# A planned single-core kernel: new fetch durations in its planner, score products that write whole PSUM banks, and a new table of priorities

## The chip, the cores and the metric

The kernel runs on one core of a Trainium2 chip. The metric is the device time of one execution in microseconds (us). A profiled execution gives its own span, from the first to the last instruction of the program. TensorE is PE in the profile, its weight loads are PEld, VectorE is DVE, ScalarE is ACT, GpSimd is POOL, and SyncE, which issues most of the transfers, is SP.

## What is computed

A retention layer (attention without softmax, with a decay for each head) is followed by two matrix products with a gate between them. There are 8 batches, 8 heads, 576 positions and 64 numbers a head, and the middle of the second part is 2048 wide. All inputs and the output are float32.

```python
scores = scale * np.matmul(q, k.transpose(0, 1, 3, 2))
Dmat = np.where(rel >= 0, gamma[:, None, None] ** rel[None, :, :], 0.0)
attn_out = np.matmul(scores * Dmat[None, :, :, :], v)
x = attn_out.transpose(0, 2, 1, 3).reshape(B * S, H * D)
h = x @ w_in
g = h * np.cos(h)
return (g @ w_out).astype(np.float32)
```

## The kernel before, in words

**The work.** The 4608 tokens are cut into 9 tiles of 512. A tile is made of two units of attention; a unit is one batch and a stretch of its positions, all 8 heads. For a unit `unit` loads k, q and v and casts them to bf16 (the decay is multiplied into q and v there, line 605), `scores` makes the products of keys and queries in PSUM and multiplies them with a triangle (line 714, on DVE), `states` adds keys times values to a running state, and `outputs` makes the attention result that becomes the tile's `xt`. All matmuls of attention are of 64 rows by 64 columns, in four lanes of the array; `emit_lanes` strings them into one task and line 675 issues them.

The first product of tiles 0 to 3 is `mlp1` (line 879), with a sine on ACT (line 888) and the gate on DVE (line 891). In tiles 4 to 8 (`SEVEN`) it is `seven1` (line 1008), which makes the same product from seven block products instead of eight, and the second product is `wino2` (line 1148) in all tiles, by the same scheme. In `seven1` one of the accumulations does not start from zero: ACT writes the first product into another PSUM bank (`seed`, line 939) and PE adds onto it.

**Marked banks.** The kernel keeps a flag for each of the 8 PSUM banks, `whole`: it is set when the last PE task that wrote the bank wrote all of it after one start. A seed that gets a bank without the flag has a dummy matmul of 512 columns put in front of it (`mark`, line 494); the planner counts 213 ns for it (`MARK`) and prefers a bank with the flag among those that are free (line 343). Before the change a score task starts anew with each of its products, so its banks don't get the flag.

**The planner.** The order of all instructions on all five engines is worked out when the kernel is built, by a list scheduler (`Graph.run`). Each task has an engine, a duration, the buffers that it needs and a priority. In each round every engine offers the task that could start first; among those within 60 ns (PE) or 40 ns (the others) of that, the lowest priority number goes (lines 300 to 302). The order found is emitted with the semaphore waits that the data need. The planned times themselves aren't emitted: an instruction starts on the chip as soon as its engine reaches it and its semaphores are there. This holds for SP's and POOL's transfers too, which stand in the order that the planner gave them.

Three pieces of the planner matter here. `FETCHES` holds, for stretches of planned time, how long a block of 256 PE instructions takes to arrive: PE asks for block k when it has seen 128 + 256k instructions and can't pass 443 + 256k before the block is there (lines 279 to 282). `SHIFT` is a string: each three characters say how many tasks to go on and what to add to that task's priority, in steps of 10 ns between -40.5 and +40.5 us (`shift`, line 226). And where the plan holds a gap of more than 400 ns on PE, while the bank for it is still free, dummy matmuls are emitted to fill it (`warm`, line 500); this ends with the first `mlp1` task of tile 1.

A task of attention is called `ses/` (scores), `ses:` and `ses+` (outputs). Going to one from another kind of task costs 95 ns in the plan, leaving one 105 ns, and one task of attention draws the next with a bonus of 2000 ns (`ENTER, LEAVE, BOND`).

Of the kernel before, what the change touches and what calls it, by code (L numbers as in the profile page):

```python
# [11 lines left out]
B, H, S, D = 8, 8, 576, 64  # L12
DM, DFF = H * D, 2048
# [6 lines left out]
NT = 72  # L20
# [79 lines left out]
def ap(t, size, p0, n, off, *dims):  # L100
    return bass.AP(t, p0 * size + off, [[size, n]] + [list(d) for d in dims])
# [29 lines left out]
class Graph:  # L131
# [54 lines left out]
    @staticmethod  # L186
    def fetch(at):
        return next(f for end, f in Graph.FETCHES if at < end)

    FETCHES = ((30000, 11500), (55000, 9500), (68000, 10200), (104000, 7800), (118000, 13000), (205000, 8800), (1e9, 6500))  # L190
    MARK = 213
    ENTER, LEAVE, BOND = 95, 105, 2000

# [181 lines left out]
class Kernel:  # L375
# [10 lines left out]
    SLABS = ((0, 'q', 0, 100), (2, 'q', 1, 101), (1, 'k', 1, 102), (3, 'k', 1, 103))  # L386
    NEXT = 2
    SHIFT = (
        "$|KLw3?#U,,G3(j'Xw'Q/$X((Oe$6_6w'8cY/cu/am-@X&h2/fT&^Z)u,'bK'Z/$Zt$X5)W0%Wo$Si)LO&Q8)V?&GC&>H&Xd&J="
        "&_;%hW$BL&Jk&Q#(Y3$CR&Ec&R3&I_&jf&Gz)Fi,Ul)X(&H\\%L3&V6'U{(R|$T'&K6&[,%Ev-0w%mf%hO'oe$fT$CQ%pN(^l+EV"  # L390
        "$8I*--'%V$=d$:1%=@$=-$Xp&.:$21&Yx$tv%kW$nq+wV*Sm)B_/?^&Ej)9[&,4&>V&LX&Wy)X+$Jj%ED$JH$WK&YT$1A)*k,#k"
        "$_*&3I+S^)PL$-y&9s$c%&-w(JS$<|&]L'LL'M.;=A&D<&;3&#`);o,Y`&U`._`,Yp'-@%VS$`j%$$$Y+<B=$N7'dd'c%$KF&;b"
        "$fO'U`,I99^#'Ym)ND'E*$FW%Jk%F\\.2@,sT$aT)W>(^T%T_'[Q.80&N0,/B-^B$A{%\\J&:0%CC-Vp+Ao,0z%i-%#U$+D%X-'Vi"
        "%XA$Bd%SJ&^d$Z#$JA)Sk'?#$@B)@;/66$F]&3H%-)%5r&+/%.q'DM&Zp0TU2M.&A\\&q-*Tc(D5'4P%Pu$5^%UZ*%M(9P$9a';>"
        "*g{-\\Z'Wt&\\K?kt&VZ'MP%p9(%B8GP(I''8c%.#$\\f(Z*;Y15J6(>n$Aa*B|*\\Y:Yg$R;%Vb$7e&_R,&i0dx6\\S'AW*E\\%Xx%RH"
        "(XU(4Z&:S7Wo.So&Se,^[&Xc-`K$L\\%Wp$XH$T++Zd'U<*|K.Y7,Mb'Ar&#b%S_%To%\\p$J\\%=#'7E$fZ$)'(/G%.<(7U)Qx$k6"
        "&2]&.U':a$2Y%8O%$b'=S'BS-_0$XW)L8$Z=+-j$,w6|C$|K9xJ"
    )
    GATE = 'k'
    TXENG = ("pool", "dve", "pool", "dve")  # L400
# [276 lines left out]
    def scores(self, u, prio, todo, split, extra=(), join=None):  # L677

        t, rem = self.tiles[u], u[1] == 2 or self.fine(u)
        kt, qt = t["kt"], t["qt"]  # L680
        N, ny = (64, 1) if rem else (128, 2)
        phases = []
        for cc in range(1 if rem else 2):
            lanes = {q: [] for q in self.LANES}
            sc, pt = [Buf("bk"), Buf("bk")], Buf("pt")
            t["pt", cc] = pt
            for r, s in self.LANES:
                n = 0
                for c in range(4) if rem else (2 * cc, 2 * cc + 1):
                    for y in range(2):  # L690
                        def rhs(r=r, s=s, c=c, y=y):
                            o = c * 128 + 64 * s
                            return ap(self.at(qt), 1024, 64 * r, 64, o + 512 * y, [1, 64]) if rem else ap(
                                self.at(qt), 1024, 64 * r, 64, o, [512, 2], [1, 64])
                        lanes[r, s].append((N, self.mm(
                            lambda r=r, s=s, n=n, sc=sc: ap(self.at(sc[r]), 512, 64 * s, 64, n * N, [1, N]),
                            lambda r=r, s=s, c=c, y=y: ap(self.at(kt), 1024, 64 * r, 64, y * 512 + c * 128 + 64 * s, [1, 64]),
                            rhs)))
                        n += 1
            reads = [(x, y) for x in (kt, qt) for y in range(2)]  # L700
            writes = [(b,) for b in sc]
            phases.append((lanes, reads, writes, []))
        for v, s in todo:
            self.states(v, s, *phases[-1][:3])
        if join is not None:
            join.append((u, phases))
            if len(join) < 2:
                return
            self.emit_lanes("ses/%d.%d" % u, prio, [x for _, y in join for x in y], alloc=[self.tiles[v]["pt", 0] for v, _ in join])
        for cc, ph in enumerate([[x] for x in phases] if split else [phases] * (join is None)):  # L710
            self.emit_lanes("ses/%d.%d" % u, prio + cc * split, ph, alloc=[t["pt", cc + x] for x in range(len(ph))])
        for b, pt, r in [(x[2][r][0], self.tiles[v]["pt", cc], r) for v, y in join or [(u, phases)]
                         for cc, x in enumerate(y) for r in range(2)]:
            self.one("dve", 610, lambda e, r=r, b=b, pt=pt: e.tensor_tensor(  # L714
                ap(self.at(pt), 1024, 0, 128, 512 * r, [64 * ny * ny, 8 // ny // ny], [1, 64 * ny * ny]),
                ap(self.at(b), 512, 0, 128, 0, [64 * ny * ny, 8 // ny // ny], [1, 64 * ny * ny]),
                ap(self.TR[ny], 64 * ny * ny, 0, 128, 0, [0, 8 // ny // ny], [1, 64 * ny * ny]), ALU.mult),
                r=[(b,)] + [("tr", ny, y) for y in range(ny)], w=[(pt, r)])
        for v, s in todo:
            self.snap(v, s)  # L720
        for i, more in enumerate(extra):
            alone = ({q: [] for q in self.LANES}, [], [], [])
            for v, s in more:
                self.states(v, s, *alone[:3])
            self.emit_lanes("ses=%d.%d" % u, prio + (split or 1000 * (i + 1)), [alone])
            for v, s in more:
                self.snap(v, s)
# [594 lines left out]
```

## Time and profile before

| | us |
|---|---|
| time, median of 3 runs | 284.11 (283.97 to 285.01) |
| profiled execution, span | 282.1 |
| PE busy | 274.2 |
| DVE busy | 226.7 |
| ACT busy | 174.9 |
| POOL busy | 152.8 |

The granted TensorE clock was 1.000 over the whole span. The transfers moved 49.90 MB. The busy time of an engine is the union of its instructions' spans. PE's matmuls are pipelined: the mean time of one matmul of 256 columns is 273 ns, but eight of them in a row took 0.87 us, so counts times distance, and not counts times mean, is what a row of matmuls costs. The seconds column of a table by windows is the length of the window; after it stand the busy times of the engines with their number of instructions.

### The profile page before, as it was taken

To read this page: it belongs to the slowest core of one execution; us is meant where nothing else is said; L and a number is where in the kernel's file an instruction comes from. 1 tells how busy PE (TensorE), PEld (TensorE's weight loads), DVE (VectorE), ACT (ScalarE), POOL (GpSimd) and SP (SyncE) were. 2 spreads that over 40 slices of the span, in tenths; PEclk is the share of its full clock that TensorE was granted. 3 is DMA by queue.
4 is the path that set the end of the run, shared out by engine and by line. 5 is a ranking of instruction groups with operands and counts; after the bars stand their busy time and mean duration, and the time that the engine had idled before them with its cause. 6 is when DMAs were issued, how large, how long until landed. Compare 5 with 4: busy or idle time off the path is not lost.

```text
span 282.1 us, 9696 instructions
## 1 busy us (share of the span) xinstructions
PE 274.2 (97%) x4088; PEld 216.5 (77%) x4088; DVE 226.7 (80%) x389; ACT 174.9 (62%) x355; POOL 152.8 (54%) x170
## 2 busy tenths in 40 slices
PE   7899999999999999999999999999999999999995
PEld 2567576888784476458888888888888889888884
DVE  4677979989937898898969786889689979579753
ACT  4357683672446744764578767785778577777620
POOL 5452870487334745258587949783779333433410
PEclk9999999999999999999999999999999999999999
DMA  7999999999999999999999999997857002200124
GB/s 194 265 224 279 244 179 228 283 199 193 192 260 224 207 188 258 188 200 188 293 159 260 184 244 207 231 208 169 169 145 151 3 2 77 77 0 2 74 77 149
DMA packets 133130, 49.90 MB, mean 177 GB/s; under 512 B 105440, under 2 KB 128992, under 8 KB 133088
## 3 DMA queue, kind: packets, MB, share of 16 engines
q1 hardware_dynamic: 128576, 44.84, 74.1%
q0 software_dynamic: 4224, 4.19, 9.3%
q8 instruction: 32, 0.52, 0.8%
q10 hardware_dynamic: 288, 0.26, 0.3%
q14 instruction: 10, 0.08, 0.1%
HBM read 36.70 MB, written 9.44 MB: 164 GB/s over the span
## 4 chain that ended last, share of the span: by engine, by line
PE 83%; DMA 8%; DVE 5%; POOL 1%; issue 1%; ACT 0%; SPq 0%; DVEq 0%
PE bk L1148 37%; PE bk L1008 22%; PE bk L879 14%; PE bk L675 8%; DMA stgv<-in_v_dram 3%; DMA wout<-in_moe_w_out_dram 3%; DVE pt L714 2%; DMA stgq<-in_q_dram 1%; PE bk L629 1%; PE bk L500 1%; DVE tw L1057 1%; POOL natv L605 1%; DVE gt L891 1%; DVE s L1079 1%; DVE s L1085 0%
## 5 line engine op out<-in xcount | busy, mean ns | idle before, releaser
L997 POOL TENSOR_TENSOR gt<-sq,cb 128x512 bf16<-128x512 f32 x40 | 46.1, 1161 | 38.5 <-ACT cb L993 24.6
L879 PE MATMUL bk<-xt,win 128*128 128x256 bf16 (+1 forms) x352 | 61.5, 321 | 0.2
L888 ACT ACTIVATE cb<-bk 128x256 bf16<-128x256 f32 (+1 forms) x88 | 41.7, 480 | 24.8 <-PE bk L879 22.6
L891 DVE TENSOR_TENSOR gt<-bk,cb 128x256 bf16<-128x256 f32 (+1 forms) x88 | 46.3, 542 | 12.5 <-ACT cb L888 8.5
L605 POOL TENSOR_TENSOR qnat<-stgq,wq 128x512 bf16<-128x512 f32 x32 | 33.5, 1051 | 39.8 <-DVE s L1079 19.9
L605 POOL TENSOR_TENSOR natv<-stgv,wv 128x512 bf16<-128x512 f32 x36 | 37.8, 1055 | 18.9 <-PE bk L675 4.3
L879 PEld LDWEIGHTS bk<-xt,win 128*128 128x128 bf16 x352 | 32.8, 98 | 19.3 <-ACT xt L555 0.8
L1148 PE MATMUL bk<-tw,s 128*128 128x256 bf16 x288 | 36.2, 273 | 0.4 <-ACT os L555 0.2
L1148 PE MATMUL bk<-wout,gt 128*128 128x256 bf16 x288 | 36.1, 273 | 0.3 <-DMA wout<-in_moe_w_out_dram 0.3
L1148 PE MATMUL bk<-wout,s 128*128 128x256 bf16 x288 | 35.9, 273 | 0.0
L997 DVE TENSOR_TENSOR gt<-bk,cb 128x512 bf16<-128x512 f32 x40 | 27.3, 687 | 9.5 <-ACT cb L993 6.9
L1008 PE MATMUL bk<-xt,win 128*128 128x256 bf16 x240 | 34.9, 273 | 0.0
L991 DVE TENSOR_TENSOR sq<-bk,sq 128x512 f32<-128x512 f32 x40 | 27.0, 686 | 9.3 <-ACT sq L555 4.3
L714 DVE TENSOR_TENSOR pt<-bk,tr 128x512 bf16<-128x512 f32 x48 | 30.7, 682 | 2.5 <-PE bk L675 2.4
L993 ACT ACTIVATE cb<-sq 128x512 bf16<-128x512 f32 x40 | 25.0, 630 | 11.3 <-DVE sq L991 11.0
L1148 PEld LDWEIGHTS bk<-tw,s 128*128 128x128 bf16 x288 | 28.0, 98 | 4.5 <-DVE tw L1057 0.3
L555 ACT ACTIVATE sn<-bk 128x512 f32<-128x512 f32 (+1 forms) x29 | 16.2, 565 | 24.0 <-PE bk L1148 22.2
L1148 PEld LDWEIGHTS bk<-wout,s 128*128 128x128 bf16 x288 | 27.6, 98 | 4.3 <-DVE gt L891 0.2
L1148 PEld LDWEIGHTS bk<-wout,gt 128*128 128x128 bf16 x288 | 27.7, 98 | 3.8 <-DMA wout<-in_moe_w_out_dram 0.5
L993 ACT ACTIVATE cb<-bk 128x512 bf16<-128x512 f32 x40 | 23.9, 600 | 8.6 <-PE bk L1008 7.2
L556 POOL CAST natk<-stgk 128x512 bf16<-128x512 f32 x34 | 20.9, 627 | 13.7 <-DMA stgk<-in_k_dram 8.4
L1137 DVE TENSOR_TENSOR os<-bk,sn 128x512 f32<-128x512 f32 (+1 forms) x28 | 18.5, 665 | 10.1 <-PE bk L1148 9.0
(80 smaller groups left out, 428.4 us busy)
## 6 DMA issues: line engine op xcount, KB each, us to landing
out_dram<-os SPq DMA_DIRECT2D x16, 512.0 KB, 4.6
stgq<-in_q_dram SPq DMA_DIRECT2D x20, 256.0 KB, 5.1
stgv<-in_v_dram SPq DMA_DIRECT2D x20, 256.0 KB, 5.0
stgk<-in_k_dram SPq DMA_DIRECT2D x20, 256.0 KB, 5.5
stgq<-in_q_dram SPq DMA_DIRECT2D x6, 512.0 KB, 6.9
stgk<-in_k_dram SPq DMA_DIRECT2D x6, 512.0 KB, 6.9
stgv<-in_v_dram SPq DMA_DIRECT2D x6, 512.0 KB, 7.2
win<-in_moe_w_in_dram POOLq DMA_DIRECT2D x4, 512.0 KB, 8.5
```

Source lines behind the costliest of these rows:

```text
L556: return self.one(eng, dur, lambda e: e.tensor_copy(dst(), src()), r=r, w=w, port=eng == "pool", **kw)
L605: self.one(eng, 610 if eng == "dve" else 1030, lambda e, out=out, inp=inp, tab=tab, col=col, hs=hs: e.tensor_tensor(out(), inp(), ap(tab, ...
L675: return lambda e: e.matmul(out(), lhs(), rhs(), start=start, stop=True, skip_group_check=True)
L714: self.one("dve", 610, lambda e, r=r, b=b, pt=pt: e.tensor_tensor(ap(self.at(pt), 1024, 0, 128, 512 * r, [64 * ny * ny, 8 // ny // ny], [1 ...
L879: inst = e.matmul(ap(self.at(bk), 512, 0, 128, 0, [1, n]), ap(self.WIN, 4 * DFF, 0, 128, c * DFF + 128 * f, [1, 128]), ap(self.at(xt), 204 ...
L888: self.one("act", n - 15, lambda e: e.activation(ap(self.at(cb), TB, 0, 128, 0, [1, n]), ap(self.at(bk), 512, 0, 128, 0, [1, n]), AF.Sin, ...
L891: self.one("dve", 75 + n / 0.96, lambda e: e.tensor_tensor(ap(self.at(gt), NF * TB, 0, 128, f * TB + 256 * h0, [1, n]), ap(self.at(bk), 51 ...
L991: self.one("dve", 610, lambda e: e.tensor_tensor(half(src), self.at(bank).ap(), half(src), ALU.add), r=[(bank,)], w=four(src))
L993: self.one("act", 530 if name else 490, lambda e: e.activation(self.at(cb).ap(), ap(self.at(src), size, 0, 128, 0, [1, 512]), AF.Sin, bias ...
L997: self.one(eng, 1120 if name else 610, lambda e: e.tensor_tensor(ap(self.at(gt), NF * TB, 0, 128, (8 * n + 2 * g) * TB + 256 * h, [TB, 2], ...
L1008: inst = e.matmul(ap(self.at(bank), 512, 0, 128, 256 * f, [1, 256]), l(c, f), rr(c), stop=True, skip_group_check=True, start=(first and f ...
L1148: inst = e.matmul(place(bank, tt), l(f, tt), rr(f), stop=True, skip_group_check=True, start=(first and f == 0 and tt < len(bank)))
```

## The change

Three things are edited. The durations of the planner's fetches are set to four stretches in place of seven:

```diff
-    FETCHES = ((30000, 11500), (55000, 9500), (68000, 10200), (104000, 7800), (118000, 13000), (205000, 8800), (1e9, 6500))
+    FETCHES = ((30000, 11500), (55000, 10200), (205000, 8600), (1e9, 6300))
```

The score products start a bank with the first product of each lane alone (`n == 0`) and write the others without a start; their tasks hand their banks over as `whole`, in the joined form for all but the banks of the running state:

```diff
-        phases = []
+        phases, banks = [], []
...
                         lanes[r, s].append((N, self.mm(
                             lambda r=r, s=s, n=n, sc=sc: ap(self.at(sc[r]), 512, 64 * s, 64, n * N, [1, N]),
                             lambda r=r, s=s, c=c, y=y: ap(self.at(kt), 1024, 64 * r, 64, y * 512 + c * 128 + 64 * s, [1, 64]),
-                            rhs)))
+                            rhs, start=n == 0)))
                         n += 1
             reads = [(x, y) for x in (kt, qt) for y in range(2)]
             writes = [(b,) for b in sc]
+            banks += sc
             phases.append((lanes, reads, writes, []))
...
-            self.emit_lanes("ses/%d.%d" % u, prio, [x for _, y in join for x in y], alloc=[self.tiles[v]["pt", 0] for v, _ in join])
+            self.emit_lanes("ses/%d.%d" % u, prio, [x for _, y in join for x in y], alloc=[self.tiles[v]["pt", 0] for v, _ in join],
+                            whole=[k[0] for _, y in join for x in y for k in x[2] if k[0] not in self.ST])
         for cc, ph in enumerate([[x] for x in phases] if split else [phases] * (join is None)):
-            self.emit_lanes("ses/%d.%d" % u, prio + cc * split, ph, alloc=[t["pt", cc + x] for x in range(len(ph))])
+            self.emit_lanes("ses/%d.%d" % u, prio + cc * split, ph, alloc=[t["pt", cc + x] for x in range(len(ph))], whole=banks)
```

And the string `SHIFT` is another one. The old one has 281 entries, up to task 1445; the new one has 1450, up to task 1450, one for nearly every task. The values of both lie between about -40 and +40 us; their standard deviation is 18.6 us in the old and 20.3 us in the new.

```diff
     SHIFT = (
-        "$|KLw3?#U,,G3(j'Xw'Q/$X((Oe$6_6w'8cY/cu/am-@X&h2/fT&^Z)u,'bK'Z/$Zt$X5)W0%Wo$Si)LO&Q8)V?&GC&>H&Xd&J="
...
+        "#B+$@($Pc$\\8$[#$M&$K8$MM$Gy$P*$j3$b/$he$bI$ML$\\|$Sb$|*$S<$I($l?$P%$m6$VJ$W%$bp$::$?A$]]$aQ$Ox$;'$P:$>)$PI"
...
     )
```

No instruction is added, removed or resized by these edits, but for the dummy matmuls, which the planner's result decides. What the new priorities decide is the order on each engine, the order of the transfers, and which of a pool's buffers each task gets.

More of the change, by code (lines that the diff above doesn't have):

```diff
@@ L388 @@
     SHIFT = (
-        "$|KLw3?#U,,G3(j'Xw'Q/$X((Oe$6_6w'8cY/cu/am-@X&h2/fT&^Z)u,'bK'Z/$Zt$X5)W0%Wo$Si)LO&Q8)V?&GC&>H&Xd&J="
[L390 to L397, printed above, removed]
+        "#B+$@($Pc$\\8$[#$M&$K8$MM$Gy$P*$j3$b/$he$bI$ML$\\|$Sb$|*$S<$I($l?$P%$m6$VJ$W%$bp$::$?A$]]$aQ$Ox$;'$P:$>)$PI"
@@ new lines @@
+        "$Ad$5Y$PY$[M$I-$|6$S4$>S$e&$Q$$c?$Kv$ci$V@$J{$JO$`p$^t$Hx$e7$4F$#-$|s$#`$8K$VN$KH$Em$>A$Ae$SB$Y)$P@$Mh$|="
+        "$V<$Sv$\\7$Rp$Tt$SL$Y-$Xs$E`$<i$K($Xw$KB$@n$*:$:q$In$U/$EQ$zb$hU$3b${D$K)$Al$Zv$HJ$Rm$#g$@J$a`$Cr$RJ$\\S$#-"
+        "${C$<q$hP$6c$X5$H:$RC$O($?1$ZB$R]$WI$'<$U;$d*$+r$p5$R+$8L$Hv$a1$bX$<\\$l5$#-$Zn$kO$Sp$;A$XT$'&$)\\$FN$5Y$_R"
+        "$E($Ml$A.$9x$c1$C)$[H$9]$.'$,<$@9$9w$+M$4=$,5$#6$WO$-y$ki$=`$)Y$EK$r_$E9$L&$Vo$3T$Ed$oF$Ef$Fk$gk$)w$`j$xF"
+        "$k?$aw$i$$iE$J>$^G$UD$D\\$Fp$TG$Mc$b#$'-$*l$N<$*+$It$DE$`1$F.$)z$=f$P5$cZ$i($Cv$c{$Ak$cU$#j$j=$g6$XO$St$Tm"
@@ new lines @@
+        "$`|$SQ$eL$^P$Wv$,\\$V8$Rc$zD$]=$cv$AW$Li$0n$Wo$k;$n7$Y1$<S$Ng$:^$Qs$`-$kV$ES$|&$0J$D=$Y)$F%$)u$>,$U]$?z$PV"
+        "$=d$lF$.h${e$8I$])$d-$O5$,+$8.$HS$Bh$Mm$.($2%$4?$1#$Iu$7E$?^$,r$SB$`c$lW$Ui$Q=$]_$7s$aH$`N$]r$c;$QF$'{$#0"
+        "$kM$T_$EO$KE$|r$MZ$aK$Lz$Q$$\\W$'3$bl$Nh$Qb$/k$?m$)3$RM${Z$9:$.a$=v$D{$VB$S:$7Y$X[$V2$#-$zZ$rS$E#$8j$/`$a="
+        "$Iy$Qr$Y&$ie$S?$s8$kj$Oq$VP$N'$*;$>Y$>o$uk$L3$WM$Iy$P.$@y$gC$ff$W&$>P$<v$ZO$K5$_1$^6$aV$j%$[n$e>$S&$0X$P+"
+        "$ZG$L_$Yu$`-$V:$zS$b`$l)${w$bD$@n$|s$'($hi$`,$-o$oH$)B$e[$TA$NB%JR$AQ$S]$\\+$fz$Cm$.P$LZ$RV$6l$k$$f)$>/$Y,"
@@ new lines @@
+        "$-_$d+$4S$Ur$gT$RQ$LI$$%$Y>$?8$6c$C@$3i$Db$JG$Ai$;{$9?$Fg$?m$5d$B,$q<$Z>$g[$T$$#-$[h$0X$Pk$W=$A-$BB$NU$3#"
+        "$M0$^;$CC$^A$8;$Y|$_m$*+$?Y$K]$[]$aC$a[$:m$2N$QB$84$up$Da$+n$H`$X<${$$B7$&6$IC$fO$3W$53$cy$-@$8v$LO$BY$lV"
+        "$x\\$hA$jn$cF$W1$Wz$s)$#-$Dp$zx$`x$AG$dX$Re$^5$A2$+L$<`$#3$)L$)4$Ly$w%$O/$DU$GK$d`$|s$-S$R|$Iu$[:$1>$]U$&$"
+        "$Ji$d\\$q9$Lf$@8$Z`$[3$y>$a:$[+$\\9$W%$U.$b`$0q$Oo$1I$OY$a]$X{$<<$?k$R{$cD$qG$R7$cD$[B$V'$])$QE$5J$H5$Vl$,L"
+        "$v|$0r$=i$HT$Cr$EI$hJ$dA$wK$c0$[5$Vl$V7$(q$AO$Vq$[]$4'$|)$DO$=%$u*$b4$0_$hD$3H$C1$\\?$@N$JV$K\\$.N$XK$f-$h="
@@ new lines @@
+        "$M%$_<$=-$OT$K[$Kj$NT$eZ$@P$(D$Xq$9&$gG$CJ$=S$Su$=v$U6$9m$lT$Iq$.Q$gL$GO$^{$Zh$oM$E@$yG$P|$RW$2,$vi$?)$Ej"
+        "$a4$(W$@X$K7$z3$YB$EB$j_$Kz$V\\$<9$a:$LB$|s$4@$^%$i{$]r$[:$`-$E5$@s$N5$rq$8>$<A$W*$ng$F;$[S$0k$<)$I6$A6$KO"
+        "$D`$M7$OG$WF$I*$F*$X,$DY$B.$Pp$]N$\\f$OW$J%$Sa$K1$]8$Y|$ZY$]F$X=$E3$DU$S[$c]$r/$v2$8m${|$nr$`6$Rv$gC$\\e$o7"
+        "$xL$Cj$QB$@U$^*$vH$PM${r$tn$Sm$Ki$:$$0^$YM$#-$b)$mh$CI$ns$\\i$5W$Yi$TQ$1x$f[$\\6$SS$6C$V/$Wf$:0$Lt$dq$Ma$I6"
+        "$qh$fg$se$Wr$`,$cn$Ou$pd$l8$zV$W.$ZR$l)$g[$KI$Ud$bV$:&$::$f8$XO$ik$w,$eS$mE$HM$T/$n'$*U$Z\\$jo$mf$QU$bR$q["
@@ new lines @@
+        "$Nq$RY$jl$F&$ZU$sc$CU$1Y$26$2t$#@$W\\$B8$f/$n8$@-$8t$-f$XU$z1$[>$Nb$tK$mT$5R$4h$]K$Pv$V:$MO$Q1$z?$/s$Y8$ZQ"
+        "$n3$|X$HS$W#$wP$[0$ps$9t$[h$Ea$C$$\\6$0)$f>$z9$=V$:h$Ul$M-$d$$]e$_A$$2$mc$gH$54$gN$t,$I)$U\\$[#$RZ$hh$d/$NP"
+        "$wx$g6$2($qR$4|$ag$i0$Kk$uj$#-$Y@$u;$_n$p:$<\\$jv$=j$GI$3T$Dl$m/$z^$56$|^$#9$^k$8z$yy$@_$O]$Sb$2$$S)$qG$=x"
+        "$T=$Qb$6q$FT$Xy$=K$TO$p,$KZ$ld$GP$P*$Du$fS$S@$5($Bv$e[$$f$N#$G+$vG$45$:1$Y?$?x$w,$)0$C;$JQ$;%$tA$L9$k_$Bf"
+        "$<F$x`$cA$AC$Vc$HI$^4$NU$sC${m$;8$J2$ba$x'$iL$N[$L%$iE$he$)^$>M$m@$1|$:/$v1$hZ$l|$DE$L/$Gw$?K$;\\$wc$lx$@H"
@@ new lines @@
+        "$,F$^m$*3$c8$`;$#2$E-$0A$M*$U2$I.$Y%$w6$ZO$ar$X+$yz$Xz${y$jt$9m$]#$4U$GF$Fp$dJ$go$H*$?u$@B$cf$SD$qh$x6$hC"
+        "$dY$74$p|$B]$C+$^;$Wa$\\:$Ru$>B$W{$V($a[$Ss$Os$F8$58$U+$OV$Xd$KA$CA$Bw$\\h$Vo$J3$F<$ck$M8$KT$BM$Rr$bp$_,$Ip"
+        "$VY$ER$fo$^W$RD$_u$IK$LW$Wz$Ha$da$=%$LP$]H${5$;k$#-$[6$AM$XK$'q$v^$KA$^?$qc$\\G$|d$>e$1`$)>$ka$>W$O%$4e$0+"
+        "$IT$QN$Q{$;_$;G$HC$+9$+a$.n$Ar$a.$uI$kD$/q$QA$TC$`a$/\\$pF$6d$^@$Bf$O]$pC$5/$[[$;=$Q{$'d$<i$C?$MA$CL$[D$hc"
+        "$sP$?n$??$g%$wF$.m$]d$cA$`#$IQ$_d$G7$vB$t{$G_$qN$O=$<L$7/$@:$j0$J^$?n$^+$>9$DR$@[$s]$Cg$SX$ph$Xn$K.$+i$YN"
@@ new lines @@
+        "$oX$TJ$a[$[k$f'$Xg$;%$m&$b*$$0$cu$1W$8-$y=$z;$04$$R$8R$U@$b`$6S$]E$Lr$f($cN$T7$ZP$|7$\\M$'$$B]$Sb$YK$z4$a&"
+        "$mH$rt$nH$iU$h?$[<$|s$|s$Db$-h$c.$5P$d%$@)$L%$ib$z#$vl$TF$k)$^_$@($?K$.E$-]$+*$uQ$nI$rr$Cb$VY$fR$wq$pS$:z"
+        "$jt$N,$04$y<$W3$|)$M|$Pp$|1$My$Gk$NA$8+$t[$8z$b+$d3$Pf$N@$z2$oP$6/$'m$Ve$8|$N($K;$1O$ON$+a$&2$Fv$O2$$^$U$"
+        "$r%$XC$&[$rl$4R$[m$8/$?t$g0$Y-$AI$NU$uv$UG$P)$@Y$Te$]'$j0$9\\$G.$LF$YU$J>$PD$yr$:J$bX$VP$C&$V\\$X\\$^p$y%$io"
+        "$hB$b)$|($v7$5A$nL$=j$^H$yn$d]$rX$>|$Ea$jQ$/|$d$$1b$mT$_/$X*$iA$j^$f|$#-$Od$O)$#>$HZ$27$CU$p3$aj$oi$#-$AA"
@@ new lines @@
+        "$f'$=Q$`($]{$;>$S($WU$|j$`k$dQ$jZ$ZJ$es$IK$`=$.w$;#$hQ$g|$bd$@/$L2$gI$US$db$u{$o_$x)$|s$yf$:g$2;$yV$fA$d5"
+        "$ZT$?A$uE$Ou$36$a^$>j$>M$*|$GI$W3$\\x$/l$4K$Vb$gI$c{$wv$q8$#6$:*$Pi${K$Vw$ZF$<K$D*$P0$]|$]`$@t$J@$Ot$hj$^X"
+        "$N>$Nv$`E$>]$gk$6W$eb$R%$kh$_P$9Q$8]$K)$Wj$U2$;_$4x$A&$cL$>V$BJ$9R$`($Sj$N;$JP$8Q$T4$RP$LW$%u$<=$2U$6r$r4"
+        "$'z$[&$#H$Z|$Tw$>D$K<$<]$D|$@_$Hf$v#$L&$|s$c]$9<$f)$Dw$&E$XJ$sg$Kp$-\\$3j$wv$b$$yJ$#?$ox$7c$lx$5D$RS$xD$Q|"
+        "$E-$`T$#-$TU$ES$4G$I.$J=$T'$`V$hr$e*$MA$^8$^?$Ol$Zl$bU$/^$VT$D5$Kr$D]$^c$0e$^7$/Q$,^$G:$M#$:3$#-$Fd$2U$%8"
@@ L398 @@
+        "$]G$Mi$8q$F[$Br$?g$TF$K2$IE$^|$5*$T]$M`$?q$d<"
     )
```

## The prediction

> **What bounds the kernel now.** I read the page's busy times first, then PE's busy time by stretches of the span, then what PE waited for, then the chain of waits of the first 60 us.
>
> ```profile
> span 282.1 us, 9696 instructions
> PE 274.2 (97%) x4088; PEld 216.5 (77%) x4088; DVE 226.7 (80%) x389; ACT 174.9 (62%) x355; POOL 152.8 (54%) x170
> ```
>
> PE is busy in all but 7.9 us of the span. No order of the same 4088 matmuls can give back more than this, the dummy matmuls among them, and the spacing inside its rows of matmuls. The window table says where the 7.9 us lie (after the window's length come PE, PEld, DVE, ACT, POOL, then clock, DMA share, GB/s):
>
> ```profile
> core 0: us, PE busy (x) PEld busy (x) DVE busy (x) ACT busy (x) POOL busy (x), PEclk, DMA share, GB/s
> 0.00:5.00 5.00, 3.88 (x9) 1.16 (x9) 1.24 (x14) 3.18 (x5) 2.39 (x16) 1.00 0.59 154
> 5.00:15.00 10.00, 8.19 (x141) 5.18 (x141) 6.99 (x12) 3.62 (x8) 4.69 (x6) 1.00 1.19 274
> 15.00:50.00 35.00, 33.34 (x529) 23.37 (x529) 28.65 (x58) 21.36 (x50) 17.14 (x21) 1.00 1.13 229
> 50.00:270.00 220.00, 219.60 (x3343) 178.77 (x3337) 185.34 (x298) 145.53 (x290) 128.61 (x128) 1.00 0.82 168
> 270.00:282.20 12.20, 9.19 (x85) 7.98 (x82) 4.45 (x9) 1.25 (x3) 0.00 (x0) 1.00 0.33 111
> ```
>
> There are three stages. Up to 50 us PE idles 1.12 + 1.81 + 1.66 us. From 50 to 270 us it idles 220 - 219.60 = 0.40 us: this stretch is a solid row of matmuls, and whatever is won before it comes out at the end unreduced, because nothing but PE sets its length. The last 3.0 us hold the end of the last tile and its store, and the edits leave their code alone. PE's own waits agree, all of them, with the longest in the last column:
>
> ```profile
> PE bk L500 <- DVE lg L526: 1.1, 1, 1.1
> PE bk L675 <- DVE pt L714: 1.0, 2, 0.9
> PE bk L629 <- DVE qnat L605: 0.7, 1, 0.7
> PE bk L675 <- POOL natv L605: 0.6, 1, 0.6
> PE bk L675 <- DVE kt L556: 0.4, 2, 0.2
> PE bk L1148 <- DMA wout<-in_moe_w_out_dram: 0.3, 1, 0.3
> PE bk L1148 <- ACT os L555: 0.2, 1, 0.2
> PE bk L1148 <- DVE tw L1057: 0.2, 1, 0.2
> ```
>
> In the chain of waits (its longest pieces: start, length, what) the early stage is a series of handovers and landings; from 46.5 us on PE matmuls carry it.
>
> ```profile
> 0.79 4.16 DMA stgq<-in_q_dram
> ...
> 9.80 2.50 DVE pt L714 x4
> ...
> 17.82 1.40 PE bk L500 x6
> 20.65 9.81 DMA stgv<-in_v_dram
> 30.54 2.04 POOL natv L605 x2
> 33.88 8.80 DMA wout<-in_moe_w_out_dram
> 46.52 1.05 PE bk L1148 x8
> ```
>
> So a v slab that is 9.81 us under way and a slab of the second weight that is 8.80 us under way set the chain from 20 to 43 us, in a stretch in which the transfers' share is 1.13, and the dummies of line 500 stand in PE's row there.
>
> **The change, part by part.** First, the banks. Before, the marks are where the score edit would save time:
>
> ```profile
> nothing on L494; most used: ['L675', 'L1148', 'L1008', 'L879', 'L84', 'L555', 'L629', 'L566', 'L888', 'L891', 'L993', 'L997', 'L605', 'L556', 'L500', 'L714', 'L991', 'L1079', 'L1085', 'L1137', 'L644', 'L1036', 'L939', 'L1307', 'L932']
> L939 ACT ACTIVATE bk<-bk x20: 579/582/619, 134.6 to 260.6; 128x512 f32<-128x512 f32 x20
> L500 PE MATMUL bk<-one x16: 379/384/634, 4.5 to 44.9; 128*128 128x512 bf16 x16
> ```
>
> Not one mark was emitted for the 20 seeds (line 939): each got a marked bank already. The score edit therefore takes away 0 x 0.23 us. The 0.23 us is a dummy of the same 512 columns in a row, 1.40 us / 6 in the chain. It issues the same matmuls with the same operands, so its own cost is zero; no row shows a product without a start in this place, and I bound it by the attention outputs (same shape, no start after the first, also line 675), whose medians are the same as the scores': 193 ns for both in these rows, so nothing either way.
>
> ```profile
> L675 PE MATMUL bk<-qt,kt x576: 186/193/313, 9.1 to 222.4; 64*64 64x64 bf16 x128, 64*64 64x128 bf16 x64
> L675 PE MATMUL bk<-pt,natv x576: 187/193/240, 12.4 to 233.4; 64*64 64x64 bf16 x128, 64*64 64x128 bf16 x64
> ```
>
> What the edit can do is indirect: with more banks marked the planner needs fewer detours for a seed. In the other direction, a new order that places seeds on unmarked banks would pay up to 20 x 0.23 = 4.7 us; the preference for marked banks and the added marks speak against it. Value taken: 0, with 0 to +4.7 as bounds.
>
> Second, the fetch durations. They emit nothing; they move planned times. Whether the planned stalls exist on the chip is read from the waits above: no wait of PE names a block of instructions, though the page lists 32 of them (32 x 256 = 8192, about PE's 4088 matmuls and 4088 weight loads).
>
> ```profile
> q8 instruction: 32, 0.52, 0.8%
> 30.00:55.00 25.00, 23.60 (x384) 17.48 (x382) 21.63 (x43) 15.05 (x34) 12.78 (x15) 1.00 1.06 225
> 68.00:104.00 36.00, 35.72 (x573) 24.56 (x574) 28.46 (x46) 19.67 (x40) 16.27 (x20) 1.00 1.12 212
> 104.00:118.00 14.00, 14.00 (x208) 8.66 (x206) 12.47 (x20) 7.80 (x16) 6.46 (x6) 1.00 1.12 218
> 118.00:205.00 87.00, 86.98 (x1419) 73.08 (x1418) 73.62 (x114) 60.36 (x121) 62.04 (x62) 1.00 1.04 210
> ```
>
> The planner lets PE go 443 - 128 = 315 instructions from the request to the block. At the pace of these rows (matmuls plus weight loads over time) that takes 315 / ((384 + 382) / 25) = 10.3 us, then 9.9 us, 10.6 us and 9.7 us. The old 13.0 us of the third stretch thus planned a stall of up to 13.0 - 10.6 = 2.4 us for each block at mean pace, and PE was busy for 14.00 of 14.00 us there. The new 8.6 us plans none at mean pace; 7.8 to 8.6 us in the second and 9.5 to 10.2 us in the first come nearer to the pace without crossing it. Direct value 0, since no stall is there to be removed. Bounds: nothing below zero, and above it what a worse order costs, which is the third part. The Trainium skill speaks against this part of the change: Runtime: NRT & Kernel Launch, section Instruction fetch mechanics, says that instructions are refilled in blocks of 256 and that crossing into the next is "mostly hidden". By that rule the planner pads against stalls that don't happen and the term is zero at best; by the planner's own reading, PE would have stalled in the third stretch. The 14.00 of 14.00 us side with the page.
>
> Third, the order. All of the time is here. Its price can't be counted instruction by instruction, because every queue is re-sorted: SP's transfers and POOL's weight transfers as well, and whoever stands behind a moved wait. I bound it by what PE doesn't use. From 15 to 50 us there are 1.66 us of idle, and the dummies:
>
> ```profile
> 15.00:50.00 35.00, 1.86 (x7) 0.60 (x7) 1.00 1.13 229
> ```
>
> They hold 1.86 us more, 3.5 us together. From 5 to 15 us there are 1.81 us of idle and the other 9 dummies, but there the chain is one unit's work in a row (q landing, its cast, its transposes, scores, triangle, outputs), with 2.50 us of DVE between two PE steps; I take 0 there. After 50 us 0.40 us can be won. In sum the order can give 0 to 3.5 + 0.4 = 3.9 us. I take half, 2.0 us, nearer to neither end: the dummies stand where PE has no work while v and weights land, and a different order of slabs moves which work is on hand, but the slabs' 512 KB each still come through a DMA share that is full. If an early slab is put later, the next things late are the scores and first products that read it, and PE idles again; that is why not all of it is taken.
>
> In the 220 us behind, the cover is DVE, ACT and POOL being ahead of PE; it is thinnest where DVE is full:
>
> ```profile
> 60.00:80.00 20.00, 19.70 (x324) 16.49 (x326) 19.55 (x35) 8.44 (x20) 10.82 (x13) 1.00 1.13 194
> ```
>
> Here DVE is busy for 19.55 of 20 us and PE loses 0.30 us.
>
> Sum: span 282.1 - 2.0 = 280.1 us. The span lies 284.11 - 282.1 = 2.0 us below the median of the runs; this part is outside of the program's order and stays. Forecast: 282.1 us.
>
> **The rivals.** *The solid stretch breaks (slower).* The old order leaves 0.40 us of idle in 220 us, so a fresh one can hardly gain there and can lose. The mechanism: a bank is handed back by DVE, ACT or POOL later than the plan says, the next PE task, which stands first in PE's row, waits, and all behind it waits too. If the whole stretch ran at the idle share of its worst part, 0.30 / 20, it would lose 3.3 us in place of 0.4; with nothing gained earlier this gives 284.1 + 2.9 = 287.0 us. It decides from the point where idle time after 50 us exceeds 0.4 us by what is gained early plus 1.4 us. For it: DVE is busy for 80% of the span, and 0.40 us leaves room on one side only. Against it: ACT is free for a third and POOL for two fifths of that stretch (145.53 and 128.61 of 220 us busy), and of PE's waits listed above a single one of 0.2 us, on ACT's line 555, lies there.
>
> *It is moved, not won (no change).* The early stage stays bound by the same landings, and the idle time turns up under other names: 15 to 50 us keeps its 3.5 us, and 284.1 us results, to within 1.4 us. For it: the chain's two long landings, 9.81 and 8.80 us, lie in transfers that have to be made in any order. Against it: dummies are emitted only where the plan itself had more than 400 ns with nothing for PE, so the plan, and not the landing alone, left the 1.86 us empty.
>
> *Marks appear.* The 20 seeds pay 4.7 us, 288.8 us. Unlikely by the preference for marked banks, under 2%; it counts as slower.
>
> **How the numbers follow.** A measurement of this kernel tells about 0.5%, 1.4 us, from no change; its three runs spread over 1.0 us. I give the early gain 0.45 (faster by over 0.5%, its own range 279.6 to 282.7 us), no change 0.20, the broken stretch 0.33 and the marks 0.02 (both slower). The two sides are this close because the early gain is bounded by 3.9 us and the loss is not. The likeliest case gives 282.1 us. The range: below, all of the 3.9 us and 0.6 us of the stage from 5 to 15 us, 284.1 - 4.5 = 279.6 us; above, the broken stretch at its price, 287.0 us, and a little of what lies past it, 287.2 us.
>
> **What would show it right or wrong.** Right: idle plus dummies of line 500 between 15 and 50 us fall from 3.5 to about 1.5 us, idle between 50 and 270 us stays under 0.5 us, no line 494 appears, line 1148 still enters the chain for good near 45 us, and the end has the same 3 us. Wrong by the second case: the same 3.5 us under other releasers. Wrong by the first rival: waits of PE on DVE or ACT between 50 and 270 us that add up to 2 us or more. The forecast also falls if the number or the spacing of PE's rows changes: more groups of line 675 between rows of 256 columns, or over 24 dummies.

## The result, and the profile after

| | before | changed | ratio, 95% interval |
|---|---|---|---|
| first comparison, median us | 284.04 | 285.35 (285.04 to 286.15) | 1.0051, 1.0028 to 1.0074 |
| the same kernel once more, median us | 283.85 | 285.56 (284.04 to 287.45) | 1.0058, 1.0027 to 1.0088 |

The changed kernel is slower, by 1.3 us, where 2.0 us less had been forecast. Medians, here and below, are over all runs of a kernel, and ratios leave out runs over 1.5% above the fastest of the same kernel. The page of the changed kernel, with the same two lines as before the change:

```profile
span 283.3 us, 9699 instructions
...
PE 272.8 (96%) x4089; PEld 214.8 (76%) x4089; DVE 228.4 (81%) x389; ACT 174.8 (62%) x355; POOL 151.4 (53%) x170
```

The span grew by 1.2 us. The median lies as far above it as before, 2.0 us (285.35 - 283.3); the profiled execution itself took 285.09 us. The windows of the changed kernel, with the columns as before:

```profile
5.00:15.00 10.00, 7.30 (x146) 4.52 (x146) 6.98 (x12) 3.90 (x8) 4.37 (x6) 1.00 1.19 274
15.00:50.00 35.00, 33.25 (x475) 23.42 (x474) 28.49 (x58) 22.25 (x53) 17.41 (x21) 1.00 1.15 234
50.00:270.00 220.00, 218.45 (x3376) 177.01 (x3374) 186.22 (x296) 143.63 (x286) 127.19 (x128) 1.00 0.80 166
270.00:283.30 13.30, 9.96 (x92) 8.68 (x89) 5.43 (x11) 1.85 (x4) 0.00 (x0) 0.95 0.35 120
```

Of these, the dummies alone between 15 and 50 us (PE and its weight loads on line 533, which was line 500):

```profile
15.00:50.00 35.00, 2.01 (x7) 0.56 (x7) 1.00 1.15 234
```

From 15 to 50 us nothing was won: 1.75 us of idle and 2.01 us of dummies, 3.8 us against 3.5. From 5 to 15 us PE idles 2.70 us in place of 1.81. That is no loss by itself: the kernel before with twenty PE instructions more, an experiment below, idles 2.65 us there at the same span of 282.1 us. From 50 to 270 us, the solid stretch, PE now idles 1.55 us in place of 0.40. These are PE's waits over the whole span, as far as they lie over 0.3 us; of them only the first row lies between 50 and 270 us:

```profile
PE bk L708 <- issue: 1.3, 2, 0.8
PE bk L533 <- DVE lg L559: 1.1, 1, 1.1
PE bk L662 <- DVE qnat L638: 1.0, 2, 0.8
PE bk L662 <- POOL natk L589: 0.8, 2, 0.5
PE bk L708 <- POOL natv L638: 0.6, 1, 0.6
PE bk L708 <- ACT kt L588: 0.5, 2, 0.3
PE bk L914 <- DMA win<-in_moe_w_in_dram: 0.4, 1, 0.4
```

The first row is new. "issue" means that the profile shows no semaphore that ended the wait. PE's timeline in the changed kernel puts the two gaps into the middle of rows of attention, between matmuls that wait for nothing (the bracket is the idle time before the row):

```profile
70.58 0.31 PE L708 MATMUL bk<-natv,natk 64*64 64x64 bf16 x12
71.48 0.31 PE L708 MATMUL bk<-natv,natk 64*64 64x64 bf16 x14 [0.60 <-issue]
...
118.76 0.21 PE L708 MATMUL bk<-qt,sba 64*64 64x64 bf16 x1
119.72 0.31 PE L708 MATMUL bk<-qt,sba 64*64 64x64 bf16 x11 [0.75 <-issue]
```

From instruction start to instruction start PE stood still for 0.79 and 0.96 us, 1.75 us together. The instruction that ends the first gap is number 1985 in PE's list and the one that ends the second is number 3521 (matmuls, weight loads and the sequencer's own waits, counted from zero in the trace). Both are 193 past a multiple of 256, and they are 6 x 256 apart.

### The profile page after: what moved, and what is told of

Read it like the earlier page. It is cut to its first block, busy times and chain, and to the rows that moved or that the text cites. A ratio compares the mean times of both kernels' runs of the same rounds, so it can differ in the third digit from the quotient of the medians.

```text
span 283.3 us, 9699 instructions
## 1 busy us (share of the span) xinstructions
PE 272.8 (96%) x4089; PEld 214.8 (76%) x4089; DVE 228.4 (81%) x389; ACT 174.8 (62%) x355; POOL 151.4 (53%) x170
## 4 chain that ended last, share of the span: by engine, by line
PE 88%; DMA 7%; SPq 1%; DVE 1%; issue 1%; POOL 1%; ACT 0%
PE bk L1183 39%; PE bk L1043 22%; PE bk L914 17%; PE bk L708 9%; DMA stgk<-in_k_dram 3%; DMA stgq<-in_q_dram 3%; SPq L599 1%; DVE pt L749 1%; PE bk L662 1%; POOL qnat L638 0%; POOL win L894 0%; POOL natk L589 0%; ACT qt L588 0%; ACT kt L588 0%; DVE os L589 0%
## 5 line engine op out<-in xcount | busy, mean ns | idle before, releaser
L914 PE MATMUL bk<-xt,win 128*128 128x256 bf16 (+1 forms) x352 | 60.4, 321 | 1.0 <-DMA win<-in_moe_w_in_dram 0.4
L923 ACT ACTIVATE cb<-bk 128x256 bf16<-128x256 f32 (+1 forms) x88 | 41.7, 480 | 22.1 <-PE bk L914 20.3
L638 POOL TENSOR_TENSOR natv<-stgv,wv 128x512 bf16<-128x512 f32 x36 | 37.3, 1043 | 14.2 <-DVE s L1120 4.9
L1183 PE MATMUL bk<-wout,gt 128*128 128x256 bf16 x288 | 36.7, 273 | 0.0
```

The lines of the kernel that those rows point to most:

```text
L638: self.one(eng, 610 if eng == "dve" else 1030, lambda e, out=out, inp=inp, tab=tab, col=col, hs=hs: e.tensor_tensor(out(), inp(), ap(tab, ...
L914: inst = e.matmul(ap(self.at(bk), 512, 0, 128, 0, [1, n]), ap(self.WIN, 4 * DFF, 0, 128, c * DFF + 128 * f, [1, 128]), ap(self.at(xt), 204 ...
L923: self.one("act", n - 15, lambda e: e.activation(ap(self.at(cb), TB, 0, 128, 0, [1, n]), ap(self.at(bk), 512, 0, 128, 0, [1, n]), AF.Sin, ...
L1183: inst = e.matmul(place(bank, tt), l(f, tt), rr(f), stop=True, skip_group_check=True, start=(first and f == 0 and tt < len(bank)))
```

## The experiments

Two theories were held against each other. *Blocks*: PE's instructions come in blocks of 256 through the same DMA engines as the data, and PE stands still when it has run through its lead (the instructions that it still has when it asks for the next block) before that block is there. *Order*: the gaps belong to their place in the new order, or the new order is worse in ways that don't hang on blocks.

**Twenty PE instructions more.** Tiny matmuls on the dummies' bank, at the start, where PE waits for q anyway, add 10 matmuls and their 10 weight loads, so every later block border falls 20 instructions earlier in the work, and the order stays. The same edit went into the kernel before.

```diff
     def warm(self, n):
+        tiny, self.TINY = self.TINY, (0, 0)
         def mm(e):
-            for _ in range(n):
+            for _ in range(n - tiny[1]):
...
+            for i in range(tiny[0]):
+                p = 64 * (i % 2)
+                inst = e.matmul(ap(self.at(self.wb), 512, p, 64, 0, [1, 64]), ap(self.ONE, 128, p, 64, 0, [1, 64]),
+                                ap(self.ONE, 128, p, 64, 0, [1, 64]), start=True, stop=True, skip_group_check=True)
...
+    TINY = (10, 0)
```

> The changed kernel with 10 tiny matmuls (64x64 by 64 columns, on the dummies' bank) behind the first nine dummies, in PE's idle gap before q lands: 20 more PE instructions, nothing else moved. Blocks theory (PE stood still at 70.7 and 118.8 us, 0.8 and 1.0 us, because the next 256 instructions had not arrived): both block borders now fall 20 instructions earlier in the program, ahead of the attention rows, both gaps go, and the time falls by about 1.7 us, from 285.35 to 283.6 us. Order theory (the two gaps belong to their place in the new order, or the order is worse all over): nothing changes, 285.4 us within 0.5, gaps at the same instructions.

> The kernel before with the same 10 tiny matmuls. Blocks theory: no border of it lies near a short lead with 20 instructions more either, so no change: 284.0 us within 0.5. Order theory: the same, 284.0 us. (The tiny matmuls cost nothing by themselves, in both.)

The kernel before with the tiny matmuls took 283.95 us, ratio 1.0004 (0.9983 to 1.0026): they cost nothing that the time shows, though its profile has a gap of 0.59 us at a border near 36 us, where none had been expected. The changed kernel went from 1.0051 to 1.0017 (0.9994 to 1.004), 284.44 us; the two intervals overlap, so here the place of the gaps tells more than the time. The gap at 119 us was gone: its block had ended 5.0 us after the request point, in place of 10.0 us. The other one had stayed, at the same instruction 1985, and had grown:

```profile
71.01 0.22 PE L716 MATMUL bk<-natv,natk 64*64 64x64 bf16 x4
72.42 0.35 PE L716 MATMUL bk<-natv,natk 64*64 64x64 bf16 x20 [1.19 <-issue]
```

The row of matmuls is cut 20 instructions earlier than before, so the gap sticks to the number of the instruction and not to the work. That it stayed and grew, to 1.38 us, was not expected: the block came 8.2 us after the request point in this execution, in place of 6.7 us.

**Ninety-six instructions more**, with `TINY = (49, 1)`, in both kernels.

> The changed kernel with 49 tiny matmuls in place of one of the first nine dummies: 96 more PE instructions. Blocks theory: by the trace of the changed kernel the borders now meet rows of attention at about 105, 122, 177 and 210 us where PE goes through its lead in less time than a block took to come; stalls add up to about 5 us instead of 1.7, and the time rises by 3 to 4 us to about 289 us (287 to 291). Order theory: 285.4 us within 0.5.

> The kernel before with the same 49 tiny matmuls in place of one dummy. Blocks theory: short leads at about 23 and 178 us, 0.3 to 0.7 us each, so 0.5 to 1.5 us slower: about 285 us; far less than the changed kernel loses with the same edit. Order theory: 284.0 us within 0.5.

The changed kernel took 285.44 us, ratio 1.0054 (1.0019 to 1.009). The gaps moved to 105.8, 122.9 and 179.0 us (0.77, 0.57 and 0.44 us), where they had been expected. None over 0.26 us stood at 210 us, one of 0.49 us stood at 24 us where none had been expected, and the time did not rise, where 3 to 4 us had been expected. The kernel before lost far more than expected: the three runs in the ratio took 285.26, 288.70 and 289.19 us, ratio 1.0141 (1.0086 to 1.0197), where about 285 us had been expected. Its profiled execution was the longest of its runs, 289.0 us of span, and isn't part of that ratio, so the lengths of its gaps are not those of the three. Its timeline has two gaps that the profile of the kernel before doesn't have:

```profile
24.63 1.13 PE L887 MATMUL bk<-xt,win 128*128 128x256 bf16 x7
28.82 1.46 PE L887 MATMUL bk<-xt,win 128*128 128x256 bf16 x6 [3.07 <-issue]
...
111.45 0.83 PE L1156 MATMUL bk<-wout,gt 128*128 128x256 bf16 x6
113.14 1.05 PE L1156 MATMUL bk<-wout,gt 128*128 128x256 bf16 x8 [0.86 <-issue]
```

These lie inside rows of full matmuls, far from any handover of attention, in the old order. The changed kernel with the same edit stops at the same two borders, instructions 705 and 3265, in a run of 285.54 us. Together with the gaps that moved in the changed kernel, this rules out the order theory for the gaps: the old order stalls as the new one does when its borders fall badly. My sizes were wrong both times. I had worked them out with a block's delivery time at another moment, and this time varies: the block of instruction 1985 ended 6.7 us after its request point in one profile of the changed kernel and 4.8 us after it in the other.

**Two loads moved back.** PE's program stays the same to the instruction; in front of each of two blocks SP issues one load of 256 KB less.

```diff
         order = self.G.run()
+        order = self.held(order)
...
+    HOLD = (('q', (3, 1), 0, 70400), ('v', (4, 1), 1, 114500))
+
+    def held(self, order):
+        to = {}
+        for which, u, half, at in self.HOLD:
+            b = self.staged[which, u]
+            t = [t for t in order if t.eng == "sp" and b in t.bufs][half]
+            to[t] = at
+        return sorted(order, key=lambda t: to.get(t, t.start))
```

> The changed kernel with two of its loads moved back on SP's queue, both with 10 us or more until their unit is used: the first half of q of unit (3,1) from 64.8 us to behind the next store (about 71 us), the second half of v of unit (4,1) from 110.7 us to behind the store at 115.5 us. PE's program is the same to the instruction. Blocks theory, with the block delayed by the transfers queued ahead of it: the blocks that came at 69.96 and 118.37 us come about 1.1 us earlier each (256 KB at some 230 GB/s), both gaps of PE all but go, and the time falls by 1.2 to 1.7 us to about 283.9 us. Order theory: PE's order is untouched, 285.4 us within 0.5, both gaps stay.

> Both remedies: the two loads moved back and the 20 PE instructions more. Blocks theory: the gap of 1.4 us that stayed at 71 us with the 20 instructions alone goes too; 283.3 us, 0.2% faster than the kernel before (ratio 0.996 to 1.000). Order theory: 285.4 us.

With the loads alone: 284.87 us, ratio 1.0028 (1.0006 to 1.005), about half of the expected gain, and its interval overlaps that of the changed kernel. The gap at 119 us is gone: the block ended 8.3 us after its request point, where it had ended 10.0 and 9.9 us after it in the two profiles of the changed kernel. The gap at 70.6 us fell from 0.79 to 0.27 us, but that isn't shown to come from the moved load: the block came 6.2 us after its request point, and without the edit it came 6.7 us after it in one profile and 4.8 us in the other. One gap of 0.30 us stands at another border, instruction 2753. With both remedies no gap over 0.26 us is left at any border, and the waits of PE between 50 and 270 us are a single row:

```profile
PE bk L727 <- POOL natk L608: 0.2, 1, 0.2
```

The windows from 50 to 130 us, first of the changed kernel, then of the one with both remedies:

```profile
50.00:130.00 80.00, 78.65 (x1224) 55.14 (x1222) 68.08 (x111) 44.49 (x92) 42.54 (x46) 1.00 1.10 218
```

```profile
50.00:130.00 80.00, 79.83 (x1237) 56.21 (x1235) 69.30 (x113) 44.46 (x92) 42.91 (x46) 1.00 1.09 212
```

Idle time falls from 1.35 to 0.17 us. The time is 284.12 us, ratio 1.0001 (0.9976 to 1.0025), an interval that lies wholly below both of the changed kernel's. The whole loss is back, and no more: the 283.3 us that I expected were not reached. What the queue looked like in front of the late block, in the changed kernel (SP's timeline; a length is what the issue took):

```profile
109.35 0.58 SPq L599 DMA_DIRECT2D stgq<-in_q_dram  x1
109.98 0.64 SPq L599 DMA_DIRECT2D stgk<-in_k_dram  x1
110.66 1.20 SPq L599 DMA_DIRECT2D stgv<-in_v_dram  x1
111.90 2.19 SPq L677 DMA_TRANSPOSE kt<-natk  x1
114.13 1.31 SPq L677 DMA_TRANSPOSE qt<-qnat  x1
```

In the kernel with the moved loads the third of these stands behind the store:

```profile
110.30 0.58 SPq L610 DMA_DIRECT2D stgq<-in_q_dram  x1
110.92 0.65 SPq L610 DMA_DIRECT2D stgk<-in_k_dram  x1
111.61 2.31 SPq L688 DMA_TRANSPOSE kt<-natk  x1
113.97 1.39 SPq L688 DMA_TRANSPOSE qt<-qnat  x1
115.41 2.11 SPq L1082 DMA_DIRECT2D out_dram<-os  x1
117.56 0.48 SPq L610 DMA_DIRECT2D stgv<-in_v_dram  x1
```

The planner's request point for that block (128 + 256k instructions seen) was passed at 108.3 us. In the changed kernel the block's packet ended at 118.37 us, with the v load moved behind the store it ended at 116.40 us, and PE didn't stop for it.

**Parts of the change alone.** The score edit on the old kernel, the old durations in the changed kernel (its first `FETCHES` line taken back), and the new durations in the old kernel. Of the score edit one line of its diff, which stands whole under "The change":

```diff
-                            rhs)))
+                            rhs, start=n == 0)))
```

> The kernel before with the score edit alone (old priorities, old durations); the planner's choice of banks shifts and with it parts of the order. No mark of 512 columns appears, and the 576 score products take the same 193 ns in the median. Blocks theory: the order meets short leads or not by chance, as its priorities were found for other banks: 284 to 287 us. Order theory: the old priorities make the time, 284.0 us within 0.7.

> The changed kernel with the old seven fetch durations in the planner, the new priorities and score edit kept; the planner sorts anew, so the order differs in many places. Blocks theory: with 10.2 us planned from 55 to 68 us and 13.0 us from 104 to 118 us no row of attention meets a short lead there, and PE has no gap without a releaser at 70 and 119 us; the time is open, since the priorities were searched for other durations, 283.5 to 287 us. Order theory: the new priorities make the time, 285.4 us within 0.7.

> The kernel before with the four new fetch durations alone (old priorities, old score products). The planner sorts anew. If a table of priorities fits only the planner it was searched with: 286 to 293 us, with waits of PE on ACT and DVE from 130 us on, as in the changed kernel with the old durations. If the durations by themselves are harmless: 284.0 us within 0.7.

The score edit alone took 283.81 us, ratio 1.0008 (0.9984 to 1.0033), with no mark and the same median of a score product:

```profile
L675 PE MATMUL bk<-qt,kt x576: 186/193/241, 8.8 to 224.6; 64*64 64x64 bf16 x128, 64*64 64x128 bf16 x64
```

In time it is harmless. Its profile is of the slowest of its runs, 286.16 us, and idles 2.0 us between 50 and 270 us with none of it given to "issue": a single profile can lose as much in ordinary waits, so the cause of the gaps rests on their places and not on their sum alone. The changed kernel with the old durations took 292.76 us, ratio 1.0299 (1.0259 to 1.034). The old kernel with the new durations has no ratio on record; the two faster of its four runs took 290.94 and 291.39 us, beside 283.85 us. In the changed kernel with the old durations there is no gap of PE at 70 or 119 us, as the blocks theory has it, but one of 1.0 us at 94.3 us and one of 0.54 us at 253.0 us, at other borders. Both time ranges given for it missed. Most of its loss comes behind that, in waits of an ordinary kind. The window from 130 to 270 us of the kernel with the old durations:

```profile
130.00:270.00 140.00, 133.48 (x2013) 113.67 (x2012) 110.86 (x173) 93.14 (x183) 80.70 (x76) 1.00 0.69 135
```

PE idles 6.5 us there, and its largest waits in this stretch are for ACT and DVE:

```profile
PE bk L1043 <- ACT bk L974: 1.8, 2, 1.2
PE bk L708 <- DVE pt L749: 1.0, 2, 0.6
PE bk L1043 <- DVE xs L967: 0.8, 1, 0.8
```

Each table of priorities made its order only together with its own durations; with the other durations the new table was 9 us and the old one 7 us slower. What the three edits are worth one by one therefore can't be added up, and no run here has the new order with the old durations.

**The changed kernel again.**

> The changed kernel as it is, looked at in another execution. Blocks theory: gaps of PE without a releaser again in the rows of attention near 70.7 and 118.8 us, behind the same instructions (1985 and 3521 of PE's list, both 193 past a multiple of 256), with other lengths from execution to execution, 0.3 to 1.5 us each; 285.3 us, ratio 1.003 to 1.007. Order theory: gaps wander to other instructions or keep their lengths.

The gap in front of instruction 3521 stood there again, 0.79 us long, from 119.06 to 119.84 us. There was none over 0.26 us in front of instruction 1985 this time: its block had come 4.8 us after the request point, in place of 6.7 us.

Over the twelve profiles, these are all borders at which PE's list stopped for more than 0.26 us (of 372; instruction number, gap in us, and how long after the end of the block's packet PE went on):

```
kernel                   instruction: gap, resumed after the block
changed                  1985: 0.79, 1.53    3521: 0.96, 1.35
changed again            3521: 0.79, 1.35
changed, 20 more         1985: 1.38, 1.52
changed, 96 more          705: 0.49, 1.46     961: 0.31, 3.85    3265: 0.77, 1.28
                         3777: 0.57, 1.38    5569: 0.44, 1.44
before, 20 more           961: 0.59, 1.33
before, 96 more           705: 3.34, 1.42    3265: 1.13, 1.34
changed, loads moved     1985: 0.27, 1.52    2753: 0.30, 1.53
changed, old durations   2753: 1.00, 1.37    7617: 0.54, 1.59
before, new durations     961: 0.74, 1.43
before; score edit alone; 20 more and loads moved: none
```

In sixteen of the seventeen PE went on 1.28 to 1.59 us after the packet's end, whatever the gap. The one that doesn't fit, 0.31 us with 3.85 us, is no stop for a block: it follows a matmul of 512 columns, and these start 0.22 us apart there anyway. Two more facts of the twelve profiles leave the blocks theory without a rival for the gaps. At none of the other 356 borders did PE pass sooner than 1.27 us after its block's packet had ended. And all fourteen waits of PE that the profiles give to "issue" stand at such a border, none elsewhere.

## Why the prediction was wrong

*Where it failed.* Two terms failed. The 2.0 us to be won by the order were not won, which is the early stage below. What turned the sign is the second part, the fetch durations: "Direct value 0, since no stall is there to be removed", and before it the reading that the old 13.0 us "planned a stall of up to 13.0 - 10.6 = 2.4 us for each block at mean pace" while PE was busy for 14.00 of 14.00 us. From this the prediction took it that no block is late. The runs showed PE standing still for 1.75 us at two borders of the changed kernel, and with both remedies the time was back at that of the kernel before. That PE had no stall in the kernel before didn't say that blocks always come in time. It said that this order, of PE and of the transfers, kept clear of late ones (one profile of each kernel):

| request point to | before | changed |
|---|---|---|
| 1985: PE has run through its lead, us | 10.18 | 7.44 |
| 1985: the block's packet has ended, us | 4.76 | 6.70 |
| 3521: PE has run through its lead, us | 12.01 | 10.42 |
| 3521: the block's packet has ended, us | 5.91 | 10.03 |

With the twenty instructions more, the blocks of the kernel before ended 5.3 and 4.5 us after the same points. So in the changed kernel PE's lead was shorter at both borders and the blocks came later, and the mean pace hid it: at mean pace, 6750 matmuls and weight loads in the 220 us from 50 us on, PE needs about 10 us for the 315 instructions between a request and its border. In the changed kernel the block let PE go on 8.23 us after the request in front of 1985, and 11.38 us after it in front of 3521. The new 8.6 us for the planned time from 104 to 118 us lies 2.8 us under the latter, and the old 13.0 us lay over it. A duration set too short can't be the whole account, though. The 8.23 us lie under the planner's 8.6 us, and the two stops of the kernel with the old durations were as quick: 6.84 us where the planner counts 7.8, and 5.87 us where it counts 6.5. No run has the new order without the new durations, so what the durations did by themselves isn't shown.

The list of waits, from which the prediction read that no block is waited for, couldn't have shown one: in none of the twelve profiles does a wait name a block, not even where 3.34 us were lost. And the sentence ahead of the prediction that an instruction starts "as soon as its engine reaches it and its semaphores are there" leaves out a condition that these runs show: it has to have arrived.

The page of the Trainium skill that I set beside this, Runtime: NRT & Kernel Launch, section Instruction fetch mechanics, calls the crossing of a block "mostly hidden". Here it cost no more than 0.26 us at most borders, 356 of 372, and up to 3.34 us at the others; the measurement decides, and I should not have let the page side with the row.

*The early stage.* "I take half, 2.0 us": idle and dummies from 15 to 50 us should have fallen from 3.5 to about 1.5 us and were 3.8 us. This step failed as well, and the rival "It is moved, not won" describes it. The sign "over 24 dummies" came too: there were 25.

*The rivals.* "The solid stretch breaks" had the side and the place (50 to 270 us) right: 1.55 us of idle in place of 0.40. Its own condition, with nothing gained early, was more than 1.8 us and was not reached. Its mechanism, a PSUM bank handed back late, was wrong: between 50 and 270 us no wait of PE on DVE, ACT or POOL is listed. Its price, 287.0 us, took the worst part of the stretch for the whole and was 1.6 us too high. That its side and its place came out, by a mechanism that it didn't name, is luck. "It is moved, not won" had given 284.1 us within 1.4 us, which 285.35 us just keeps to; but it counted on idle time under other names in the early stage, and not on stops after it.

*What held.* The score edit takes away no mark and costs nothing (ratio 1.0008 alone). "Marks appear" did not happen in the changed kernel: its 25 matmuls of that kind are all dummies of line 533, the last at 23.1 us. The 2.0 us outside of the span stayed. 285.35 us lies in the stated range, which was 7.6 us wide; that isn't to the credit of the mechanism.

*What stays open.* No run tells which of the three edits brought the stops. With the gaps gone the changed kernel is as fast as the one before, ratio 1.0001, though its profiled span with both remedies, 281.7 us, is 0.4 us shorter than the 282.1 us before. Whether its order holds a small gain of its own can't be told at this spread. Why one and the same block comes 4.8 us after its request point in one execution and 6.7 us in another of the same kernel (gaps of 0 and 0.79 us in front of instruction 1985) wasn't tried either. That it waits behind the loads is shown for one border at most, by one profile.

## What to carry to other kernels

In a kernel whose PE never waits, the absence of a stall can be a property of the order: before costing a limit at nothing, look for what the order does to avoid it, and measure the lead at its shortest place, not at mean pace. A gap of PE that the profile gives to "issue" in the middle of a row is a candidate for a late block of instructions; whether such gaps share one number modulo 256 tells, and a few cheap instructions at the start, or a bulk load moved out of the block's way, are a test and a remedy. A table of priorities belongs to the constants it came with: here the same table with other constants cost 7 to 9 us.

## What the runs showed of the hardware

In the sixteen stops of these profiles PE waits for a block in front of instruction 449 + 256k of its list, counted from zero at the first in the profile. It goes on 1.28 to 1.59 us after the block's packet of 16 KB has ended, and at none of the other 356 borders did it pass sooner than 1.27 us after that. From the planner's request point, 315 instructions earlier, to going on it took 5.9 to 14.2 us in these stops: longest before 37 us (11.2 to 14.2 us), shortest at 253 us in the changed kernel with the old durations. PE stops where it runs through its lead in less than that. In the one profile with a load of 256 KB less in front of it, the block of instruction 3521 ended 8.3 us after its request point in place of 10.0 and 9.9 us, and the gap of 0.96 and 0.79 us was gone.
